# Cross-covariance attention with a mixture of adapters: gate weights and A in one tile, seven fillers fewer

## The chip, the cores and the metric

The kernel runs on one core of a Trainium2 chip. The metric is the device time of one execution in microseconds (us). Shown are the median of three runs and one execution taken by the hardware profiler. The engines are PE (TensorE, matrix products; PEld is its weight load), DVE (VectorE), ACT (ScalarE), POOL (GpSimd, which here mainly issues the loads) and SP (SyncE, which here issues the stores). Sixteen DMA engines move data.

## The reference

For each of 4 batches, q, k and v are 6400 x 256. The columns of q and k are normalised over the 6400 rows, a 256 x 256 attention comes out of them, and v is multiplied with it. Each of the 25600 result rows then goes through a mixture of 8 adapters of rank 16, of which the gate picks two.

```python
qn = q / (norm(q, axis=1) + 1e-6);  kn = k / (norm(k, axis=1) + 1e-6)
a  = softmax(kn.transpose(0, 2, 1) @ qn / tau)          # 4 x 256 x 256
x  = (v @ a).reshape(25600, 256)
logits = x @ w_gate                                     # 256 x 8
w  = softmax over the two largest logits of each row
out = x + sum over the two experts e: w_e * (x @ A[e]) @ B[e]
```

## The kernel before

Rows are handled in 50 chunks of 128 per batch; v comes in five tiles of ten chunks. The loads (q, k, v) turn fp32 into bf16 on the way and are issued by POOL in the fixed order of `WORDS`; SP issues the stores. A planner (`Plan`) simulates the engines with estimated costs and writes out a fixed order of steps for every engine, with the buffers that each step takes and gives back. Stores of the first batches are held back until given loads have landed (`HOLD`), so that loads go first.

Per batch there are three stages:

- G (lines 752 to 760): PE accumulates k'q and, for some groups of chunks, the squared norms. For the other groups (`OFF`) ACT squares and DVE adds up (`sq`, L775; `add`, L782; `red`, `n2p`).
- The attention: `n2`, `rsqrt`, `rq_ps`, `s`, `exp`, `aT_ps`, `aT`, then `waA_ps`. The last one multiplies the transposed attention with the gate weights (8 columns) and with A (128 columns: 8 experts of rank 16), so that each row of v needs one product for its logits and its adapter inputs. It is scaled into `waA_sb` by DVE (L910) and ACT (L908).
- The tiles of v: PE transposes (`T`, L942), `ZL` (L966) multiplies with `waA_sb` (136 columns), DVE works out the gate and its product with Z (`Ze`, L1044), PE transposes that (`gzT`, L1056), `Y` (L1069 and L1074) adds v times attention and the adapters' output, ACT and DVE copy the result to the y slots, and SP stores it.

The weights come from one step, `wts`, on DVE in the middle of the first batch: L677 copies A into a tile `a_raw` (per partition: expert, half of the 256 rows, rank), L680 the gate weights into a tile `wg_raw`, L682 scales B.

The fillers are steps `("warm", n)`, matmuls of 512 columns whose result nobody reads. The planner puts them into gaps of PE in the first batch; a number in `NO_WARM` is planned and then not emitted:

```python
def do_warm(s, n):
    if n in NO_WARM:
        return
```

Thirty are planned before PE's last real step; 12 are in `NO_WARM`, so 18 run. `keep_weights` drops a weight load if the same weights are already loaded and the load carries no semaphore, which is why the second matmul of a `waA_ps` pair has none in most cases.

Of the kernel before, what the change touches and what calls it, by code (L numbers as in the profile page):

```python
# [12 lines left out]
BF16 = mybir.dt.bfloat16  # L13
# [455 lines left out]
PARTS = {(0, 0): ((0, 5), (5, 12), (17, 8)), (0, 1): ((25, 17), (42, 8)), (3, 1): ((25, 17), (42, 8))}  # L469
REST, REST_AT, FULL, SIDE = (0, 1), 40, 112, 5  # L470
SLOTS = ((0, 4), (32, 34), (4, 6), (8, 12), (40, 42), (28, 32), (60, 62), (64, 68), (96, 98), (92, 96), (124, 126))
NO_WARM = {6, 7, 8, 9, 10, 11, 12, 25, 26, 27, 28, 29}
FINE = {3: ((0, 6), (6, 4)), 4: ((0, 4), (4, 4), (8, 2))}
SPLIT, SHARES = set(), ()
OFF = {(0, 0, 'k'), (0, 0, 'q'), (0, 1, 'k'), (0, 2, 'k'), (0, 2, 'q'), (0, 3, 'k'), (0, 4, 'k'), (0, 4,
# [102 lines left out]
def kernel(  # L578
# [11 lines left out]
    nc = tc.nc  # L590

    B, N, C = q.shape
    P = 128
    CC = C // P
    E = moe_w_gate.shape[1]
    R = moe_A.shape[2]
    ER = E * R
# [14 lines left out]
    const = ctx.enter_context(tc.tile_pool(name="const", bufs=1))  # L612
# [5 lines left out]
    W = {}  # L618
# [48 lines left out]
    def bank(s, name, shape, dtype):  # L667
        held["bank", name] = psum.tile(shape, dtype, tag=f"bank{at['bank', name]}", name=name[0] + "_ps")
        return held["bank", name]
# [2 lines left out]


    def do_wts(s):
        W["A"] = const.tile([P, E, CC, R], BF16, name="a_raw")
        for g in range(4):
            nc.vector.tensor_copy(W["A"][g * (P // 4):(g + 1) * (P // 4)], W["A0"][:, :, CC * g:CC * g + CC, :])  # L677
        W["wg"] = const.tile([P, CC, E], BF16, name="wg_raw")
        for g in range(4):
            nc.vector.tensor_copy(W["wg"][g * (P // 4):(g + 1) * (P // 4)], W["wg0"][:, g])  # L680
        W["B"] = const.tile([P, C], BF16, name="ball")
        nc.vector.tensor_scalar(out=W["B"], in0=W["B0"], scalar1=0.5, scalar2=None, op0=OP.mult)  # L682

# [206 lines left out]
    def do_waA_ps(s, b):  # L890
        ps = bank(s, ("waA", b), [P, CC, E + ER], FP32)
        for ic in range(CC):
            for cc in range(CC):
                lhsT = st[b]["aT"][:, cc, ic * P:(ic + 1) * P]
                nc.tensor.matmul(
                    ps[:, ic, 0:E], lhsT, W["wg"][:, cc, :],
                    start=(cc == 0 and ic == 0), stop=False, skip_group_check=True)
                nc.tensor.matmul(
                    ps[:, ic, E:E + ER], lhsT, W["A"][:, :, cc, :],
                    start=False, stop=(cc == CC - 1 and ic == CC - 1), skip_group_check=True)  # L900

    def do_waA(s, b, ic):
        if "waA" not in st[b]:
# [25 lines left out]
# [3 lines that stand above are left out]
        nc.tensor.matmul(bank(s, ("warm", n), [P, 512], FP32), W["ident"], W["ident"][:, None, :].to_broadcast([P, 4, P]),  # L932
                         start=True, stop=True)
# [146 lines left out]
    def do_store(s, b, i, c, n):  # L1080
# [3 lines left out]
        for rows in SHARES if (b, i) in SPLIT else (P,):  # L1084
            r = nc.sync.dma_start(out_v[b, p:p + rows, lo:lo + n, :], Y[p:p + rows, at_y:at_y + n, :])
            if (b, i) in HOLD and not p:
# [4 lines left out]


    do = dict(load=do_load, wts=do_wts, sq=do_sq, add=do_add, red=do_red, n2p=do_n2p, warm=do_warm, cast=do_cast, G=do_G, accs=do_accs, n2=do_n2, rsqrt=do_rsqrt, rq_ps=do_rq_ps, s=do_s,
              exp=do_exp, recip=do_recip, aT_ps=do_aT_ps, aT=do_aT, waA_ps=do_waA_ps, waA=do_waA,
              a=do_a, ZL=do_ZL, ZLe=do_ZLe, T=do_T, Te=do_Te, log=do_log, loge=do_loge, Z=do_Z, Ze=do_Ze, gzT=do_gzT,
              gzTe=do_gzTe, Y=do_Y, Ye=do_Ye, store=do_store)
# [55 lines left out]
```

## Time and profile before

| | |
|---|---|
| median of 3 runs | 251.62 us (251.37 to 251.63) |
| profiled execution, whole | 251.61 us |
| its span, first to last instruction | 247.2 us |
| mean granted clock of PE | 0.965 |
| busy, us | PE 215.3, DVE 185.4, ACT 169.6, POOL 27.4 |
| HBM read, written | 79.90 MB, 26.21 MB |
| waA_ps, 8 columns (L895) | 16 matmuls, 167 ns each in the middle |
| waA_ps, 128 columns (L898) | 16 matmuls, 216 ns each in the middle |
| fillers (L932) | 18 matmuls from 9.9 to 53.6 us, 13 weight loads |

The span holds the instructions only; the last transfers end after it. The duration of one matmul counts its way through the array, so matmuls in a row overlap, and what one costs is read from start to start. A window is a stretch of the span, with each engine's busy time and number of instructions in it, the clock that PE was granted (1.00 is full), and the DMA engines' mean busy share. Besides the printed views, the trace holds a record of every DMA packet with its queue, size, start and duration.

### The profile page before, as it was taken

How to read it: one execution, taken by the hardware profiler on the slowest of the kernel's cores; microseconds unless marked ns; L12 is line 12 of the kernel's file. 1: busy time of each engine (PE TensorE's matmuls, PEld its weight loads, DVE VectorE, ACT ScalarE, POOL GpSimd, SP SyncE). 2: the span in 40 equal slices, each digit the busy share in tenths (PEclk: the TensorE clock that was granted, in tenths of full speed). 3: DMA queues.
4: the chain of work that ended last, by engine and by line, in shares of the span. 5: the costliest groups of instructions: out<-in, count | busy, mean ns of one | idle time of the engine just before them, and what ended most of it. 6: DMA issues, size and time to landing. Idle time of an engine off the chain costs nothing.

```text
span 247.2 us, 5383 instructions
## 1 busy us (share of the span) xinstructions
PE 215.3 (87%) x2226; PEld 178.8 (72%) x2033; DVE 185.4 (75%) x514; ACT 169.6 (69%) x316; POOL 27.4 (11%) x61
## 2 busy tenths in 40 slices
PE   0657199398998999999969999999999999999995
PEld 0255077167777998978959787999775799999974
DVE  1145578467879789999974899998989588878780
ACT  3844442275666769888776787999443699888885
POOL 7800200200030011000201003110000000000000
PEclk9999869679999999999997999999999999999999
DMA  8999999999999999999999999999999999999999
GB/s 275 219 208 217 213 224 222 208 215 224 206 221 220 208 214 225 216 215 208 258 280 269 326 268 203 216 218 226 305 220 319 394 356 274 326 430 434 407 423 415
DMA packets 9157, 66.27 MB, mean 268 GB/s; under 512 B 1231, under 2 KB 1615, under 8 KB 5420
## 3 DMA queue, kind: packets, MB, share of 16 engines
q0 software_dynamic: 5872, 38.67, 75.2%
q1 hardware_dynamic: 2924, 26.47, 25.9%
q10 hardware_dynamic: 336, 0.79, 0.8%
q8 instruction: 17, 0.28, 0.4%
q14 instruction: 8, 0.07, 0.1%
HBM read 79.90 MB, written 26.21 MB: 429 GB/s over the span
## 4 chain that ended last, share of the span: by engine, by line
DMA 39%; PE 34%; DVE 11%; issue 9%; ACT 6%; POOL 1%; POOLq 0%; ACTq 0%
DMA v<-in_v_dram 27%; PE Y_ps L1069 10%; DMA qk<-in_q_dram 7%; PE Y_ps L1074 5%; PE ZL_ps L966 5%; DMA qk<-in_k_dram 5%; PE T_ps L942 5%; DVE ssq L782 4%; PE acc L752 3%; PE gzT_ps L1056 3%; DVE gz L1044 3%; ACT sq L775 3%; PE acc L756 2%; ACT y L922 1%; DVE y L924 1%
## 5 line engine op out<-in xcount | busy, mean ns | idle before, releaser
L752 PE MATMUL acc<-qk 128*128 128x256 bf16 (+1 forms) x400 | 75.7, 283 | 17.6 <-DMA qk<-in_k_dram 9.4
L782 DVE TENSOR_TENSOR ssq<-ssq,sq 128x1280 f32<-128x1280 f32 (+1 forms) x35 | 52.1, 1489 | 19.4 <-ACT sq L775 19.4
L752 PEld LDWEIGHTS <-qk 128*128 128x128 bf16 (+1 forms) x400 | 39.1, 103 | 31.8 <-DMA qk<-in_k_dram 11.5
L922 ACT COPY y<-Y_ps 128x512 f32<-128x512 f32 x87 | 50.7, 594 | 15.3 <-PE Y_ps L1074 13.0
L775 ACT ACTIVATE sq<-qk 128x1280 f32<-128x1280 bf16 (+1 forms) x35 | 44.8, 1280 | 23.3 <-DVE ssq L782 20.8
L1069 PE MATMUL Y_ps<-a_bf,vT 128*128 128x256 bf16 x400 | 60.0, 272 | 0.1
L1069 PEld LDWEIGHTS <-vT 128*128 128x128 bf16 x400 | 38.3, 98 | 5.1 <-issue 0.4
L1074 PE MATMUL Y_ps<-ball,gzT 128*128 128x256 bf16 x200 | 38.2, 273 | 0.0
L1044 DVE TENSOR_TENSOR gz<-zl,gatega 128x256 bf16<-128x256 f32 x95 | 35.5, 446 | 0.5
L756 PE MATMUL acc<-qk 128*128 128x128 bf16 (+1 forms) x170 | 32.6, 225 | 0.0
L942 PE MATMUL T_ps<-ident,v 128*128 128x128 f32 x200 | 26.9, 282 | 4.4 <-DMA v<-in_v_dram 4.1
L760 PE MATMUL acc<-qk 128*128 128x128 bf16 (+1 forms) x200 | 28.0, 222 | 0.0
L942 PEld LDWEIGHTS T_ps<-ident,v 128*128 128x128 f32 x200 | 22.6, 145 | 5.7 <-issue 4.3
L966 PE MATMUL ZL_ps<-waA_sb,vT 128*128 128x136 bf16 x380 | 26.3, 223 | 0.4 <-ACT y L922 0.3
L922 ACT COPY vT<-T_ps 128x512 f32<-128x512 f32 (+1 forms) x47 | 23.0, 546 | 5.2 <-PE T_ps L942 4.9
L966 PEld LDWEIGHTS <-vT 128*128 128x128 bf16 x380 | 23.8, 98 | 1.4 <-issue 0.4
L922 ACT COPY zl<-ZL_ps 128x408 f32<-128x408 f32 (+1 forms) x50 | 19.9, 457 | 3.5 <-PE ZL_ps L966 3.4
L1056 PE MATMUL gzT_ps<-ident,gz 128*128 128x128 f32 x100 | 20.0, 283 | 2.0 <-DVE gz L1044 1.9
L760 PEld LDWEIGHTS <-qk 128*128 128x128 bf16 (+1 forms) x200 | 18.5, 99 | 4.3
L1074 PEld LDWEIGHTS <-gzT 128*128 128x128 bf16 x200 | 19.5, 98 | 2.3
L924 DVE COPY zl<-ZL_ps 128x272 f32<-128x272 f32 (+1 forms) x26 | 12.7, 499 | 6.8 <-PE ZL_ps L966 6.6
L709 POOL DMA_DIRECT2D qk<-in_q_dram x11 | 6.2, 559 | 105.0 <-ACT y L922 41.3
(93 smaller groups left out, 226.1 us busy)
## 6 DMA issues: line engine op xcount, KB each, us to landing
out_dram<-y SPq DMA_DIRECT2D x10, 1280.0 KB, 11.0
out_dram<-y SPq DMA_DIRECT2D x4, 2560.0 KB, 17.6
v<-in_v_dram POOLq DMA_DIRECT2D x14, 640.0 KB, 27.4
qk<-in_q_dram POOLq DMA_DIRECT2D x5, 1600.0 KB, 16.4
qk<-in_k_dram POOLq DMA_DIRECT2D x5, 1600.0 KB, 23.4
v<-in_v_dram POOLq DMA_DIRECT2D x3, 1280.0 KB, 28.5
out_dram<-y SPq DMA_DIRECT2D x3, 512.0 KB, 5.0
qk<-in_q_dram POOLq DMA_DIRECT2D x1, 1088.0 KB, 18.2
```

The costliest lines, as they stand in the source:

```text
L752: nc.tensor.matmul(acc[ic][:, 0:256], kt[0:r, j, ic::CC], qt[0:r, j, :], start=c == 0, stop=False, skip_group_check=True)
L756: nc.tensor.matmul(acc[ic][:, 256:384], kt[0:r, j, ic::CC], kt[0:r, j, ic::CC], start=False, stop=False, skip_group_check=True)
L760: nc.tensor.matmul(acc[ic][:, 384:512], qt[0:r, j, ic * P:(ic + 1) * P], qt[0:r, j, ic * P:(ic + 1) * P], start=False, stop=c == NC - 1, s ...
L775: nc.scalar.activation(out[0:r, 0:n, :], t[0:r, j:j + n, :], ACT.Square)
L782: nc.vector.tensor_tensor(out=t, in0=t, in1=held["sq", (w, b, g), ""][0:r, 0:n, :], op=OP.add)
L922: nc.scalar.copy(out, in_)
L942: nc.tensor.matmul(ps[:, j, :], vt[:, c + j, :].bitcast(FP32), W["ident32"], is_transpose=True, start=(j == 0), stop=(j == n - 1))
L966: nc.tensor.matmul(ps[:, j, :], vT_of(b, i, c + j)[:, :, ic], st[b]["waA"][:, ic, :], start=(j == 0 and ic == 0), stop=(j == n - 1 and ic ...
L1044: nc.vector.tensor_tensor(out=pairs[:, h].rearrange("p c (e r) -> p c e r", e=E), in0=z[:, 2 * h:2 * h + 2, :].rearrange("p c (e r) -> p c ...
L1056: nc.tensor.matmul(ps[:, j, :], pairs[:, j * P:(j + 1) * P], W["ident32"], is_transpose=True, start=(j == 0), stop=(j == n // 2 - 1))
L1069: nc.tensor.matmul(ps[:, j, :], vT_of(b, i, c + j)[:, :, ic], st[b]["a"][:, ic, :], start=(j == 0 and ic == 0), stop=False, skip_group_che ...
L1074: nc.tensor.matmul(ps[:, j, :], pair[:, :, j], W["B"], start=False, stop=(j == 1), skip_group_check=True)
```

## The change

The tiles for A and the gate weights become one tile `wgA` with, for each half of the rows, 8 columns of the gate and then 128 of A. The copies of `wts` write into parts of it. In `waA_ps` the two matmuls of each step become one of 136 columns. `NO_WARM` gets the numbers 0 to 5 and 24, so that 11 fillers run. The planner's costs and its order stay.

```diff
-NO_WARM = {6, 7, 8, 9, 10, 11, 12, 25, 26, 27, 28, 29}
+NO_WARM = {0, 1, 2, 3, 4, 5, 6, 7, 8, 9, 10, 11, 12, 24, 25, 26, 27, 28, 29}
...
     def do_wts(s):
-        W["A"] = const.tile([P, E, CC, R], BF16, name="a_raw")
+        W["wgA"] = const.tile([P, CC, E + ER], BF16, name="wga_raw")
         for g in range(4):
-            nc.vector.tensor_copy(W["A"][g * (P // 4):(g + 1) * (P // 4)], W["A0"][:, :, CC * g:CC * g + CC, :])
-        W["wg"] = const.tile([P, CC, E], BF16, name="wg_raw")
+            rows = slice(g * (P // 4), (g + 1) * (P // 4))
+            nc.vector.tensor_copy(W["wgA"][rows, :, E:].rearrange("p cc (e r) -> p e cc r", e=E),
+                                  W["A0"][:, :, CC * g:CC * g + CC, :])
         for g in range(4):
-            nc.vector.tensor_copy(W["wg"][g * (P // 4):(g + 1) * (P // 4)], W["wg0"][:, g])
+            nc.vector.tensor_copy(W["wgA"][g * (P // 4):(g + 1) * (P // 4), :, 0:E], W["wg0"][:, g])
...
                 lhsT = st[b]["aT"][:, cc, ic * P:(ic + 1) * P]
                 nc.tensor.matmul(
-                    ps[:, ic, 0:E], lhsT, W["wg"][:, cc, :],
-                    start=(cc == 0 and ic == 0), stop=False, skip_group_check=True)
-                nc.tensor.matmul(
-                    ps[:, ic, E:E + ER], lhsT, W["A"][:, :, cc, :],
-                    start=False, stop=(cc == CC - 1 and ic == CC - 1), skip_group_check=True)
+                    ps[:, ic, :], lhsT, W["wgA"][:, cc, :],
+                    start=(cc == 0 and ic == 0), stop=(cc == CC - 1 and ic == CC - 1), skip_group_check=True)
```

## The prediction

> **What bounds the kernel.** I read the page first: the busy shares, the slices, the queues.
>
> ```profile
> span 247.2 us, 5383 instructions
> ...
> PE 215.3 (87%) x2226; PEld 178.8 (72%) x2033; DVE 185.4 (75%) x514; ACT 169.6 (69%) x316; POOL 27.4 (11%) x61
> ...
> DMA  8999999999999999999999999999999999999999
> ...
> q8 instruction: 17, 0.28, 0.4%
> ```
>
> No compute engine is full, but the DMA row is 9 in all slices but the first. So the 16 DMA engines are the bound. The chain of waits agrees up to 130 us (DMA v 27.1%, most of it there) and names PE after that, up to "244.64 0.59 ACT y L922". Which of the two sets the end shows in the windows of the last microseconds (PE, PEld, DVE, ACT, POOL busy, then clock, DMA share, GB/s):
>
> ```profile
> 245.00:245.50 0.50, 0.00 (x0) 0.00 (x0) 0.00 (x0) 0.23 (x1) 0.00 (x0) 1.00 0.97 393
> ...
> 247.50:248.00 0.50, 0.00 (x0) 0.00 (x0) 0.00 (x0) 0.00 (x0) 0.00 (x0) 0.50 0.96 381
> 248.00:248.50 0.50, 0.00 (x0) 0.00 (x0) 0.00 (x0) 0.00 (x0) 0.00 (x0) 0.50 0.81 315
> 248.50:249.00 0.50, 0.00 (x0) 0.00 (x0) 0.00 (x0) 0.00 (x0) 0.00 (x0) 0.50 0.26 98
> 249.00:249.50 0.50, 0.00 (x0) 0.00 (x0) 0.00 (x0) 0.00 (x0) 0.00 (x0) 0.50 0.05 20
> 249.50:250.00 0.50, 0.00 (x0) 0.00 (x0) 0.00 (x0) 0.00 (x0) 0.00 (x0) 0.50 0.03 12
> ```
>
> The last store is issued at 245.25, and the DMA engines stay full until 248: PE could end some 0.1 us earlier or later and nothing would move. From 249.0 the share is 0.05, one engine of sixteen (0.06). The time hangs on that engine.
>
> Its story is in the trace's packet records (a packet starts where the one before it on the same engine ended). Fifteen engines finish their part of the last store between 247.87 and 248.93; one finishes at 249.77. That one had a store boundary at 244.06 and the next, eight packets on, at 246.62: 2.56 us, where the others need 1.25. In between lies a 16 KB packet of queue q8, from 244.84 to 245.81: the last of the 17 instruction fetches of the page. So this fetch cost its engine 2.56 - 1.25 = 1.31 us, and without it that engine would have ended at 249.77 - 1.31 = 248.46, inside the pack.
>
> The profiled execution took 251.61 us, 1.84 more than the last packet's end on the span's clock; the median of the runs shown is 251.62, so sums made against the one hold for the other. About 0.2% (0.5 us) is what a measurement can tell from no change.
>
> **Part 1: one matmul of 136 columns.** Now a pair of matmuls with one weight load:
>
> ```profile
> 202.71 0.17 PE L895 MATMUL waA_ps<-wg_raw,aT_sb 128*128 128x8 bf16 x1
> 202.74 0.22 PE L898 MATMUL waA_ps<-a_raw,aT_sb 128*128 128x128 bf16 x1
> 202.80 0.17 PE L895 MATMUL waA_ps<-wg_raw,aT_sb 128*128 128x8 bf16 x1
> ...
> 203.04 0.57 PE L966 MATMUL ZL_ps<-waA_sb,vT 128*128 128x136 bf16 x7
> ```
>
> From start to start four pairs take 0.33 us (202.71 to 203.04). The nearest row for the merged one is ZL, also 136 columns with a weight load each: 20 in 1.18 us, 0.059 each, so four take 0.24. Bounds: 0.057 (128 columns, L760) to 0.083 (the pair, no gain). Saved: 0.09 us per batch, 0.38 in all. At 203 it lies on PE's chain, which runs without a gap to 244.6, so the last store is issued 0.09 us earlier, into DMA queues that are full until 248. Worth nothing: the cover is those full queues; if the stores kept up with PE, it would be worth 0.09.
>
> **Part 2: the copies.** The same eight DVE casts (L677 four at 0.282 us, L680 four at 0.165) now write rows of 136. Element counts stay; the A copies still write runs of 16, so I take no change. A faster copy has no reason, and the upper bound is a_bf (L916), 256 scattered elements in 0.69 us: +0.4 each, +1.6 us at 33.58. Behind them on DVE are the sums of squares up to 41.88, and behind those n2p on PE and the load that POOL issues at 42.68. That load's first packet comes at 53.5, and the first q load needed 3.9 us from issue to packet (1.44 to 5.32), so 53.5 - 42.68 - 3.9 = 6.9 us of cover. DVE itself then waits 2.23 us for ACT (acc_sb), which waited for a landing at 43.2. So nothing of it reaches the end. No wait, DMA or queue order is added.
>
> **Part 3: the fillers.** Of 18 fillers in the trace (L932) go the six at 9.85 to 12.39 and the last at 53.62. The last frees 0.22 us of PE; PE then idles at 61.0 for 1.2 us anyway. What the six do is in windows cut at the clock's steps (its changes lie at 11.59, 28.66, 35.49, 45.72, 52.55: multiples of 3.41 apart; the 1.00 before 11.59 only means that no record came earlier, since 256 columns took 0.21 us there, half speed):
>
> ```profile
> 8.18:11.59 3.41, 3.40 (x14) 1.58 (x11) 0.00 (x0) 3.41 (x3) 3.10 (x5) 1.00 1.01 207
> 11.59:15.01 3.42, 1.96 (x18) 1.08 (x15) 1.49 (x1) 1.15 (x2) 0.99 (x2) 1.00 1.05 213
> ...
> 28.66:32.07 3.41, 1.84 (x12) 0.94 (x8) 1.49 (x1) 1.85 (x2) 0.00 (x0) 0.50 1.05 215
> 32.07:35.49 3.42, 3.42 (x23) 2.35 (x18) 3.20 (x10) 1.33 (x2) 0.00 (x0) 0.50 1.07 223
> ```
>
> A window with 3.4 us of PE raised the clock at its end, one with 1.84 didn't. Without the six, 8.18:11.59 holds 2.1 us (the ten G matmuls), so the clock stays at half until 18.42, after a full window. By then PE has done 2.3 of the 3.6 us of G work that begins at 13.85; the rest ends at 19.7 instead of 17.4, the work fed at 18.72 at 22.0 instead of 21.0, the side rows at 24.4 instead of 23.6. PE next waits for a load until 30.23, and the only load that waits for these buffers (POOL, 26.78) is released by ACT at 26.5. Cost: nothing, with 2 us of cover or more. "TensorE: Matmul & The Clock Gate" (the section on why it matters for kernels) speaks against the removal: it asks for no PE gap over about 3 us between bursts; by it the slow stretch costs, and the rows above say that the cost ends in front of a DMA wait.
>
> **Part 4: what is left, the length of PE's stream.** 16 matmuls go, with three second weight loads (L898 PEld x3), seven fillers and three weight loads of theirs (the six have two, the last one its own): 29 of PE's 4314 records (2226 matmuls, 2033 weight loads, 54 semaphore instructions, a drain). The 17 fetches come 257 records apart on average: 202 records had started at the first, 4314 at the last, (4314 - 202) / 16. So fetches follow the stream, and the 17th came when PE had 38 records less than 17 * 256 = 4352. "Runtime: NRT & Kernel Launch" (Instruction fetch mechanics) gives 256 instructions per block, which agrees, and calls a crossing "mostly hidden"; by that rule part 4 is worth 0, while the tail above shows 0.84 us not hidden.
>
> Say fetch n is asked for when record 256n - o is reached. PE stood at record 202 from 23.4 to 30.2 while the first packet came at 24.95, so o is 54 or more, or less if PE's front reads ahead of a matmul that waits. With o = 54 the delays from asking to packet have a median of 1.5 us, with 67 of 2.1, with 90 of 3.3; the nearest measured delay, a store's issue to its first packet, is 3.4 to 3.6 us (116.93 to 120.48), so I stop at 90. The new stream ends at 4314 - 29 = 4285, the 17th request is at 4352 - o: beyond the end if o is below 67. Then PE ends, drains, and waits with the rest for the stores, and the fetch is gone or comes too late to matter. DMA then ends at the next engine's 248.93: **249.77 - 248.93 = 0.84 us off**, 250.8.
>
> **The rivals.**
> - A, the fetch falls out: 251.61 - 0.84 = 250.8; with the scatter of the runs (0.26) 250.5 to 251.1. For it: record 4352 already lies 38 past the end of the old stream, and will lie 67 past the end of the new one.
> - B, it still comes, 29 records later, at some 20 records per us 1.4 us later, at 246.3. Its engine still has work until 248.46, so it pays 1.31 again: 251.6, no change. This holds for o of 67 to 90, and for a front that reads on past PE's end.
> - C, it comes on another engine, of those that end at 248.2 to 248.93: end 249.5 to 250.24, 251.3 to 252.1.
> - D, the slower side: the fillers did hold the clock. If PE stays at half from 13.85 on, G ends at 48.7 instead of 42.05; the 42.68 load has its 6.9 us, but the attention and the first tile start 3.5 us late, and with one more half window (1.7 us) 5.2. They release the load that POOL issues at 70.02, whose first packet is due at 77.7: cover 77.7 - 70.02 - 3.9 = 3.8 us. It decides from a slip of 3.8 us on, price up to 1.4, middle 0.8: 252.4. Against it: from 30.23 G alone, without fillers, brought the clock back at 35.49.
>
> **How the numbers follow.** o between 54 and 67 is about a third of 54 to 90; reading ahead (o lower) adds to A unless the front also passes PE's last wait. I give A 0.48, B 0.32, C 0.10, D 0.10. The forecast is A's 250.8. Range 250.5 to 252.1: it holds A, B and C and leaves D out. Faster by over 0.2% is A without its upper edge: 0.46; slower is D with a rest of B and C: 0.13; within 0.2%: 0.41. A's own range is 250.5 to 251.1.
>
> **What would show it.** Right: q8 with 16 packets (0.26 MB) in the page, DMA share 0.00 after 249.0, PE 2203 matmuls, one waA row of 136 columns at 0.06 us start to start, half clock at 13.85 with G done before 30.23. B shows as 17 packets and again one engine (0.05) up to 249.7; C as 17 with another end. Wrong altogether: a DMA share below 0.9 for several us around 53 or 77, which would be D, or a tail set by PE.

## The result, and the profile after

The kernel after takes 250.66 us (median of six runs, 250.52 to 251.01), the kernel before 251.64 us in six runs beside it (251.37 to 251.92). The ratio is 0.9961, with a 95% interval of 0.9949 to 0.9974: 0.98 us, or 0.4%, faster. The profiled execution took 250.69 us, 0.92 less than that of before. The forecast was 250.8.

The page of the kernel after, the lines that answer to those of before:

```profile
span 245.0 us, 5349 instructions
...
PE 213.6 (87%) x2203; PEld 178.1 (73%) x2024; DVE 185.4 (76%) x514; ACT 169.0 (69%) x316; POOL 27.6 (11%) x61
...
DMA  8999999999999999999999999999999999999999
...
q8 instruction: 16, 0.26, 0.4%
```

The DMA row is as full as before, DVE, ACT and POOL are as busy as before, and the queue of instruction fetches has 16 packets where it had 17. PE has 23 matmuls and 9 weight loads less. The last windows (PE, PEld, DVE, ACT, POOL busy, then clock, DMA share, GB/s):

```profile
245.00:245.50 0.50, 0.00 (x0) 0.00 (x0) 0.00 (x0) 0.00 (x0) 0.00 (x0) 1.00 0.98 401
247.50:248.00 0.50, 0.00 (x0) 0.00 (x0) 0.00 (x0) 0.00 (x0) 0.00 (x0) 0.68 0.96 385
248.00:248.50 0.50, 0.00 (x0) 0.00 (x0) 0.00 (x0) 0.00 (x0) 0.00 (x0) 0.50 0.85 328
248.50:249.00 0.50, 0.00 (x0) 0.00 (x0) 0.00 (x0) 0.00 (x0) 0.00 (x0) 0.50 0.18 66
249.00:249.50 0.50, 0.00 (x0) 0.00 (x0) 0.00 (x0) 0.00 (x0) 0.00 (x0) 0.50 0.00 0
```

Up to 248.5 this is, within 0.04 of the DMA share, the table of before. The 0.05 and 0.03 that one engine gave from 249.0 on are gone: the last packet ends at 249.015 instead of 249.771, 0.76 us earlier. The rest of the 0.92 us is what lies behind the last packet: 250.69 - 249.02 = 1.67 us here, 1.84 before.

The two edits themselves, in the rows of the timeline (start, us from first start to last end, engine, line, operation) and of the windows cut at the clock's steps:

```profile
201.21 0.40 PE L896 MATMUL waA_ps<-wga_raw,aT_sb 128*128 128x136 bf16 x4
201.45 1.35 PE L964 MATMUL ZL_ps<-waA_sb,vT 128*128 128x136 bf16 x20
```

```profile
15.26 0.63 PE L753 MATMUL acc<-qk 128*128 128x256 bf16 x2
15.68 0.42 PE L761 MATMUL acc<-qk 128*128 128x128 bf16 x2
15.90 0.63 PE L753 MATMUL acc<-qk 128*128 128x256 bf16 x2
...
19.49 0.38 PE L753 MATMUL acc<-qk 128*128 128x256 bf16 x2
19.70 0.28 PE L761 MATMUL acc<-qk 128*128 128x128 bf16 x2
19.82 0.38 PE L753 MATMUL acc<-qk 128*128 128x256 bf16 x2
```

```profile
12.16:15.57 3.41, 1.57 (x10) 1.26 (x11) 1.53 (x2) 1.27 (x1) 0.55 (x1) 1.00 1.03 208
15.57:18.98 3.42, 3.42 (x21) 2.62 (x20) 2.08 (x2) 1.27 (x1) 0.00 (x0) 1.00 1.12 218
18.98:22.40 3.42, 3.42 (x40) 3.06 (x37) 2.08 (x2) 1.27 (x1) 0.00 (x0) 1.00 1.05 217
```

The four merged matmuls take 0.24 us from start to start (201.21 to 201.45). Without the early fillers the same four matmuls of G take 0.64 us from start to start at 15.26 and 0.33 at 19.49, and PE gets through 21 matmuls in the full window before 18.98 and 40 in the one behind it: it ran at half speed until then. (The clock column says 1.00 for the early windows in both kernels; it has no record there.)

### The profile page after: what moved, and what is told of

Its sections match the earlier page's. It is cut to its first block, busy times and chain, and to the rows that moved or that the text cites. A ratio compares the mean times of both kernels' runs of the same rounds, so it can differ in the third digit from the quotient of the medians.

```text
span 245.0 us, 5349 instructions
## 1 busy us (share of the span) xinstructions
PE 213.6 (87%) x2203; PEld 178.1 (73%) x2024; DVE 185.4 (76%) x514; ACT 169.0 (69%) x316; POOL 27.6 (11%) x61
## 4 chain that ended last, share of the span: by engine, by line
DMA 39%; PE 37%; DVE 9%; issue 8%; ACT 6%; POOL 1%; POOLq 0%; ACTq 0%
DMA v<-in_v_dram 27%; PE Y_ps L1067 11%; DMA qk<-in_q_dram 7%; PE Y_ps L1072 5%; PE ZL_ps L964 5%; PE T_ps L940 5%; DMA qk<-in_k_dram 5%; DVE ssq L783 4%; PE acc L753 4%; PE gzT_ps L1054 3%; ACT sq L776 3%; DVE gz L1042 2%; PE acc L757 2%; ACT y L920 1%; POOL qk L710 1%
## 5 line engine op out<-in xcount | busy, mean ns | idle before, releaser
L753 PE MATMUL acc<-qk 128*128 128x256 bf16 (+1 forms) x400 | 77.5, 290 | 18.1 <-DMA qk<-in_k_dram 9.6
L753 PEld LDWEIGHTS <-qk 128*128 128x128 bf16 (+1 forms) x400 | 39.9, 105 | 31.0 <-DMA qk<-in_k_dram 10.3
L757 PE MATMUL acc<-qk 128*128 128x128 bf16 (+1 forms) x170 | 32.6, 225 | 0.0
L940 PE MATMUL T_ps<-ident,v 128*128 128x128 f32 x200 | 25.8, 274 | 4.5 <-DMA v<-in_v_dram 4.2
L761 PE MATMUL acc<-qk 128*128 128x128 bf16 (+1 forms) x200 | 28.7, 227 | 0.0
L940 PEld LDWEIGHTS T_ps<-ident,v 128*128 128x128 f32 x200 | 21.7, 141 | 5.8 <-issue 4.4
L761 PEld LDWEIGHTS <-qk 128*128 128x128 bf16 (+1 forms) x200 | 19.1, 102 | 4.9
```

Of the source, the lines that this page charges most:

```text
L753: nc.tensor.matmul(acc[ic][:, 0:256], kt[0:r, j, ic::CC], qt[0:r, j, :], start=c == 0, stop=False, skip_group_check=True)
L757: nc.tensor.matmul(acc[ic][:, 256:384], kt[0:r, j, ic::CC], kt[0:r, j, ic::CC], start=False, stop=False, skip_group_check=True)
L761: nc.tensor.matmul(acc[ic][:, 384:512], qt[0:r, j, ic * P:(ic + 1) * P], qt[0:r, j, ic * P:(ic + 1) * P], start=False, stop=c == NC - 1, s ...
L940: nc.tensor.matmul(ps[:, j, :], vt[:, c + j, :].bitcast(FP32), W["ident32"], is_transpose=True, start=(j == 0), stop=(j == n - 1))
```

## The experiments

**What is in question.** The theory from the tail of the trace: the 17th instruction fetch made one DMA engine late, and the kernel after is faster only because its PE stream is too short to ask for that fetch. The rivals: PE has less to do, or ends earlier; the fillers, and with them the clock, matter; the merged matmul matters on the path.

The runs use the edits in `NO_WARM` and a pad, matmuls of one column into a PSUM bank that nobody reads, put in the place of a filler that isn't emitted:

```diff
     def do_warm(s, n):
+        if n == 0:
+            ps = bank(s, ("warm", n), [P, 512], FP32)
+            for x in range(33):
+                nc.tensor.matmul(ps[:, x % 512:x % 512 + 1], W["ident"], W["ident"][:, 0:1],
+                                 start=True, stop=True)
+            return
         if n in NO_WARM:
             return
```

**The stream's length alone.** e1: the kernel after, with that pad, in time in which PE waits for a load (10.45 to 11.46 us), so that its stream is as long as that of before, to one record.

> The changed kernel with 33 one-column matmuls and two weight loads on PE at 10 us, where PE is idle: PE's stream has 4315 records again (4314 before, 4280 changed). Fetch theory: 17 packets in q8, the last near 244, one DMA engine alone after 249.0, time back to 251.6 (ratio 0.999 to 1.002). Rival, the saved PE work counts: 33 columns in idle time cost nothing, 250.7 (ratio 0.996), whatever q8 says.

Measured: 251.79 us (251.57 to 252.09, 11 runs) against 251.88 of before (29 runs beside it); ratio 0.9996 (0.9987 to 1.0004). One microsecond of idle PE time, filled at 10 us, takes back the whole gain. The windows at the end:

```profile
249.00:249.50 0.50, 0.00 (x0) 0.00 (x0) 0.00 (x0) 0.00 (x0) 0.00 (x0) 0.50 0.09 37
249.50:250.00 0.50, 0.00 (x0) 0.00 (x0) 0.00 (x0) 0.00 (x0) 0.00 (x0) 0.50 0.05 20
250.00:250.50 0.50, 0.00 (x0) 0.00 (x0) 0.00 (x0) 0.00 (x0) 0.00 (x0) 0.50 0.03 12
```

The 17th fetch is back (its packet at 243.17), and so is one engine at a share of 0.05, up to 250.28. PE's last matmul began at 242.56 in this run, 1.8 us before that of the kernel before: PE's end doesn't set the time.

**The shorter stream by another way.** e2: the kernel before, with its pairs and two tiles, but no filler at all.

```diff
-NO_WARM = {6, 7, 8, 9, 10, 11, 12, 25, 26, 27, 28, 29}
+NO_WARM = set(range(30))
```

> The kernel before (pairs of matmuls stay) with none of the 18 fillers: 4279 records, one fewer than the changed kernel. Fetch theory: 16 packets in q8, last DMA packet near 249.0, 250.7 (ratio 0.995 to 0.998). Rival, the saved PE work counts: nothing of the merge is in it, so 251.5 or, where the fillers held the clock, slower: 251.6 to 253.0.

Measured: 250.81 us (250.78 to 251.19); ratio 0.9965 (0.9953 to 0.9978). Without the merged matmul it is as fast as the kernel after: 16 packets on q8, last DMA packet at 249.39.

```profile
q8 instruction: 16, 0.26, 0.4%
```

```profile
249.00:249.50 0.50, 0.00 (x0) 0.00 (x0) 0.00 (x0) 0.00 (x0) 0.00 (x0) 0.50 0.04 16
249.50:250.00 0.50, 0.00 (x0) 0.00 (x0) 0.00 (x0) 0.00 (x0) 0.00 (x0) 0.50 0.00 0
```

**Each half alone.** e3: the kernel after with the old `NO_WARM`. e4: the kernel before with the new one.

> The merged matmul with all 18 fillers: 4295 records. Fetch theory: time follows q8, 250.7 with 16 packets, 251.6 with 17; by my o of 54 to 90 the limit is somewhere between 4281 and 4298 records, so either can come. Rival, saved PE work: 0.09 us per batch at most, 251.3 to 251.6, whatever q8 says.

> Only the seven fillers gone, pairs of matmuls stay: 4299 records. Fetch theory: time follows q8, 251.6 with 17 packets (likelier), 250.7 with 16. Rival, the fillers matter by PE work or clock: 251.4 without them, or up to 252.4 if they held the clock, whatever q8 says.

Measured: both fall into two groups. e3: two runs at 250.73 and 250.75, nine from 251.46 to 252.44 (median 251.65, ratio 0.9992, 0.998 to 1.0005). e4: four runs from 250.75 to 251.09, eight from 251.37 to 252.04 (median 251.56, ratio 0.9985, 0.9975 to 0.9996). The groups lie where the times with and without the 17th fetch lie. So neither half brings the gain surely, and the same program can fall on either side. That its faster runs did without the 17th fetch is read from their times alone: one run of each kernel has a trace, and those of e3 and e4 are slower ones. The profiled run of e3 was of the slower group (251.78), and its page shows 16 packets; the packet records have the 17th, at 250.81, behind the stores:

```profile
248.50:249.00 0.50, 0.00 (x0) 0.00 (x0) 0.00 (x0) 0.00 (x0) 0.00 (x0) 0.50 0.27 102
249.00:249.50 0.50, 0.00 (x0) 0.00 (x0) 0.00 (x0) 0.00 (x0) 0.00 (x0) 0.50 0.02 8
249.50:250.00 0.50, 0.00 (x0) 0.00 (x0) 0.00 (x0) 0.00 (x0) 0.00 (x0) 0.50 0.00 0
250.00:250.50 0.50, 0.00 (x0) 0.00 (x0) 0.00 (x0) 0.00 (x0) 0.00 (x0) 0.50 0.00 0
250.50:251.00 0.50, 0.00 (x0) 0.00 (x0) 0.00 (x0) 0.00 (x0) 0.00 (x0) 0.50 0.15 33
```

The stores were through at 249.17, as in the kernel after. Then 1.6 us of nothing, and a fetch. The run ended 251.78 - 249.17 = 2.61 us behind the last store, where the kernel after needs 1.67: a fetch that comes too late for the stores is paid behind them, 0.94 us.

**Where the edge lies.** e5 and e6: the kernel after with pads of 4 and of 9 (each brings two weight loads with it), 4286 and 4291 records where the kernel after has 4280.

> The changed kernel with four one-column matmuls and two weight loads more: 4286 records. The padded kernel of 4315 and the ones of 4295 and 4299 fell back to 251.6 in most runs; in the one of 4295 the 17th fetch came at 250.81, after the stores, and the end waited for it. Theory: a request that falls behind PE's last wait is paid in full at the end, one that falls behind the whole program isn't. 4286 lies between: 250.7 with 16 packets if its request still falls behind the program, 251.6 with a 17th after 250. Rival, only a fetch that delays the stores counts, and the slow runs of 4295 were such: 250.7.

> The same with nine one-column matmuls: 4291 records. Late-fetch theory: the limit lies between 4280 and 4295, so 4291 is likelier past it than 4286: 251.4 to 251.8 with a fetch after 250; 250.7 with 16 packets otherwise. Rival, only a fetch among the stores counts: 250.7.

Measured: e5 again in two groups, six runs from 250.59 to 250.92 and four from 251.59 to 252.16 (median 250.90, ratio 0.9976, 0.9958 to 0.9993); its profiled run (251.59) is of the slower group and has the late fetch, at 250.77. e6: 251.81 us, all ten runs above 251.5 (ratio 0.9999, 0.9989 to 1.0009), with the fetch at 244.91. So with such pads the edge lies some 6 records above the kernel after. Request 17 comes at record 4352 - o; with the edge at about 4286, o is about 66, an estimate. The number of records alone doesn't place the edge: 4291 had no fast run in ten, while 4295 (e3) had two in eleven and 4299 (e4) four in twelve.

**No fillers at all.** e7: the kernel after with `NO_WARM = set(range(30))`, 4260 records.

> The changed kernel without the 11 fillers that it kept: 4260 records, a weaker clock between 42 and 53. Fetch theory: still 16 fetches, 250.7, nothing more to win. Rival, every PE record less is worth something: 20 records less than 4280, at 0.9 us for the 34 of the change, would give 250.2. Clock theory: the kept fillers shorten the first attention, slower without, 251 to 252.

Measured: 250.72 us (median of seven runs, 250.58 to 251.20; an eighth, at 263.72, is not counted); ratio 0.9955 (0.9944 to 0.9967). No gain and no loss against the kernel after's 0.9961: the eleven fillers that are left do nothing for the time. PE's last matmul began at 244.29 here, 1.5 us later than in the kernel after, and the stores were through at 249.23: once more PE's end is not the bound.

**One fetch more.** e8: the kernel after with pads of 153 (n = 0) and 136 (n = 6), 4573 records and 18 fetches.

> The changed kernel with 289 one-column matmuls in PE's idle time of the first batch (153 at 10 us, 136 at 24 us): 4573 records, so 18 fetches, the last again near the end. Fetch theory: the end is that of the latest engine, so 18 fetches cost what 17 do if the 18th comes to another engine: 251.6 to 251.9; 253.0 if to the same. Rival, each fetch delays the whole (1.31 us on one of sixteen engines, or about 0.9 each): 252.5. The matmuls themselves are hidden: G is late by 0.5 us at 14 and early enough for the load at 30.

Measured: 251.66 us (251.43 to 252.02); ratio 0.9993 (0.9983 to 1.0003). The 18th fetch comes at 244.71, where the 17th of before did, and 18 cost no more than 17.

```profile
248.50:249.00 0.50, 0.00 (x0) 0.00 (x0) 0.00 (x0) 0.00 (x0) 0.00 (x0) 0.50 0.47 184
249.00:249.50 0.50, 0.00 (x0) 0.00 (x0) 0.00 (x0) 0.00 (x0) 0.00 (x0) 0.50 0.10 41
249.50:250.00 0.50, 0.00 (x0) 0.00 (x0) 0.00 (x0) 0.00 (x0) 0.00 (x0) 0.50 0.11 41
```

But the share is 0.10 where one engine gave 0.05: by the packet records two engines end at 249.94 and 249.96, and the next one at 248.99.

**Is it the place of the fetch, or its number?** Up to here it could be that a fetch costs only if it falls among the last stores. e9 and e10 put the 17th far ahead of them: pads of 150 (n = 0), and of 150 and 45 (n = 0 and 6).

> The kernel after with 150 one-column matmuls and two weight loads more in idle PE time of the first batch: 4432 records on PE, so 17 fetches again (record 4352 is passed), but the 17th is asked for 118 records earlier than in the kernel before, and its packet is expected near 238 us, while all sixteen engines still have several us of loads and stores ahead. Theory (a fetch costs only where its engine can no longer give the work to the others' pace, in the last stores): about 250.8 us, +-0.3, with DMA share 0.00 after 249.3. Rival 1 (every fetch costs its engine 1.3 us to the end of the kernel, wherever it lies near the end): 251.6 to 251.8, like the kernel before. Rival 2 (the number of fetches counts, 17 against 16): also 251.6 to 251.8.

> The same with 195 one-column matmuls: 4479 records on PE, 17 fetches, the 17th asked for 165 records before the end of the stream that the kernel before has, packet expected near 236 us. Theory (only a fetch in the last stores, or behind them, costs): 250.8 +-0.3. Rival (the count, or any late fetch): 251.6 to 251.8. Between the two: if e9 is slow and this one fast, the fetch's engine needs more than about 10 us to catch up, and the boundary lies between 236 and 238 us.

Measured: 251.78 us both (251.31 to 252.21 and 251.44 to 252.22); ratios 0.9999 (0.999 to 1.0008) and 1.0000 (0.9991 to 1.0009). The theory missed: the fetch lay at 236.87 and at 236.49, and cost as much as at 244.84. In e9 its packet took 0.96 us and the 10 KB packet behind it 0.74 instead of 0.39, 1.31 us together, and thirteen us later one engine is still late:

```profile
248.50:249.00 0.50, 0.00 (x0) 0.00 (x0) 0.00 (x0) 0.00 (x0) 0.00 (x0) 0.50 0.30 115
249.00:249.50 0.50, 0.00 (x0) 0.00 (x0) 0.00 (x0) 0.00 (x0) 0.00 (x0) 0.50 0.06 25
249.50:250.00 0.50, 0.00 (x0) 0.00 (x0) 0.00 (x0) 0.00 (x0) 0.00 (x0) 0.50 0.06 25
250.00:250.50 0.50, 0.00 (x0) 0.00 (x0) 0.00 (x0) 0.00 (x0) 0.00 (x0) 0.50 0.06 25
```

A steady 0.06 is one engine of sixteen, up to 250.54. The packet records suggest why it doesn't catch up: between 10 and 240 us all sixteen engines have a packet under way all the time, in before, after, e9 and e10 alike, and the packets of q0 (the loads) take 185.8 us per engine in each of them. The data packets of every size come in multiples of sixteen, which fits a fixed share for each engine. So no engine has a pause to make up a loss in, and in e9 and e10 what it lost at 236 it still lacks at the end.

That leads to a new theory: sixteen fetches hit sixteen engines once each, in turn, and delay them alike; the 17th and 18th hit an engine a second time.

**Fifteen and nineteen.** e12 leaves out ten of the fifty chunks of G in every batch (its transfers are all there):

```diff
         acc = st[b]["acc"]
+        if c < NC - 1 and c % 5 == 3:
+            return
         (qt, j), (kt, _) = qk_of("q", b, c), qk_of("k", b, c)
```

e11 is the kernel after with pads of 180, 190, 110 and 60 (n = 0, 6, 18, 21); the last two stand in place of fillers that ran.

> The kernel after without the part of G that the chunks 3, 8, 13 and so on of each batch give (ten of fifty; their loads stay, the output differs): 4006 records on PE, 274 less, so 15 fetches. All transfers are those of the kernel after, and PE has less to do. Theory (fetches in turn over sixteen engines): one engine is early by one fetch and the others set the end as before: 250.7 us, like after, within 0.3. Rival 2 (each fetch costs time, and the last most): 249.4 to 249.9. Rival 3 (PE's end sets the time after all): some 2.5 us of PE work gone in every batch, 249 or less.

> The kernel after with 540 one-column matmuls (and four weight loads) more, spread over four stretches in which its PE waits or runs fillers: 4822 records on PE, so 19 fetches (4352 + 512 - about 64 is passed, 4352 + 768 isn't). New theory after e9 and e10, whose 17th fetch lay 8 us ahead of PE's end and cost the same: every engine is busy from the first load to the last store and cannot make a loss good, each fetch takes one engine about 1.3 us, and the fetches go round the sixteen engines in turn, so that sixteen delay all alike, and the 17th, 18th and 19th each make one engine late by one more fetch. So: 251.7 us, no more than with 17 or 18, and a DMA share of about 3/16 = 0.19 in the stretch where one engine gave 0.06 and two gave 0.10 to 0.11. Rival 1 (the fetches fall on engines at random): three late engines at most, but with sixteen fetches some engine would have had two as well, and here one may have three: up to 253. Rival 2 (each further fetch costs time): 252.5 to 253.

e12 measured: 250.94 us (250.81 to 251.16), ratio 0.9967 (0.9955 to 0.9979): as with sixteen, though PE has 274 records and 11 us of work less.

```profile
PE 202.5 (82%) x2049; PEld 168.1 (68%) x1904; DVE 185.5 (76%) x514; ACT 168.3 (69%) x316; POOL 27.6 (11%) x61
...
q8 instruction: 15, 0.25, 0.4%
```

The packet records have one engine that is early: it ends at 247.20, the next at 247.97, the middle at 248.70. So with one fetch less than sixteen one engine is early and the time doesn't move, as the new theory says; and PE's work is not the bound. (The early engine alone is weak evidence: e9, with 17 fetches, has one that ends at 247.75, the next at 248.31.)

e11 measured: 252.77 us (252.67 to 254.65), ratio 1.0064 (1.0037 to 1.009), slower than both. That is not the 251.7 of the new theory but the 252.5 to 253 of rival 2, and the picture isn't three late engines either: seven end between 249.96 and 251.11, and the middle of the sixteen, 248.52 to 248.71 in the other kernels, is 249.22. Something else went with it: in the packet records e11 alone of the fourteen kernels has engines without a packet in mid-kernel (1.2 engine-microseconds between 70 and 80, 0.8 between 90 and 100), so some load was issued late, and its q0 packets took 186.6 us per engine instead of 185.8. The pads at 48 and 52 us lie ahead of the first attention on PE, which fits a late load, but that was not traced through. For the number of fetches e11 decides nothing: neither the new theory nor rival 2 is shown by it.

**All runs by the packet records.** "Middle" is the median over the sixteen engines of the end of their last store. "Run" is the time of the profiled execution, to which the row belongs.

| kernel | fetches | last fetch at | PE's last matmul | middle | last engines | run |
|---|---|---|---|---|---|---|
| e12 | 15 | 232.84 | 243.35 | 248.70 | 249.32 | 250.99 |
| after | 16 | 232.09 | 242.75 | 248.54 | 249.02 | 250.69 |
| e2 | 16 | 231.89 | 242.72 | 248.62 | 249.39 | 251.09 |
| e7 | 16 | 234.41 | 244.29 | 248.58 | 249.23 | 250.90 |
| e3 | 17 | 250.81 | 242.46 | 248.61 | 249.17 | 251.78 |
| e5 | 17 | 250.77 | 242.71 | 248.59 | 249.13 | 251.59 |
| before | 17 | 244.84 | 244.33 | 248.52 | 249.77 | 251.61 |
| e1 | 17 | 243.17 | 242.56 | 248.58 | 250.28 | 252.09 |
| e4 | 17 | 243.46 | 242.63 | 248.57 | 249.74, 250.33 | 252.04 |
| e6 | 17 | 244.91 | 244.04 | 248.59 | 250.46 | 252.20 |
| e9 | 17 | 236.87 | 242.56 | 248.62 | 250.54 | 252.21 |
| e10 | 17 | 236.49 | 242.70 | 248.64 | 250.55 | 252.22 |
| e8 | 18 | 244.71 | 244.37 | 248.71 | 249.94, 249.96 | 251.70 |

The execution ends 1.67 to 1.84 us behind the last engine in every row but those of e3 and e5 (2.61 and 2.46), where the fetch stands behind the stores: the time follows the last engine, run by run. PE's end wanders over 1.9 us without any effect; the middle stays within 0.2 us; the last engine is 0.5 to 0.8 us behind the middle where up to sixteen fetches come before the stores are through (e3 and e5 among them), and 1.25 to 1.9 us with more. The profiled runs of e1, e6, e9 and e10 are the slowest of theirs; by the medians the 17th fetch costs about 1 us. e4 does not fit the plain count: it has a second engine 1.2 us behind with 17 fetches.

**What stays open.** That the fetches go round the engines in turn is inferred from these ends: the records don't name an engine, and no engine can be followed through the whole run. The durations of the fetch packets speak for a fixed order: in the kernel before the first eight took 975, 974, 961, 893, 893, 948, 945 and 921 ns, the next eight 974, 974, 961, 893, 879, 934, 931 and 925, and the 17th 968. They can't tell a round of eight from one of sixteen. Why e4 shows a second late engine, and why kernels of 4286, 4295 and 4299 records are sometimes fast and sometimes slow while the one of 4291 was slow ten times, was not settled. And whether sixteen fetches together cost their 1.3 us as well (all engines late alike) was not tried: it would need a PE stream without fetches.

## Why the prediction was right

- **The bound and the last engine.** Right: the table shows that the time follows the last DMA engine, and e1 and e7 that PE's end doesn't matter.
- **Part 1.** The 0.059 us per merged matmul, from the ZL row, was 0.060, and worth nothing at the end, as e2 shows, which lacks it.
- **Part 2.** The copies take 0.282 and 0.166 us, as before. Right, and the bound of +1.6 us was not used.
- **Part 3.** Half speed lasted to 18.98 (18.42 foreseen), that G stretch ended at 24.3 (24.4), and PE next waited for a load until 30.68. e7 shows that the other fillers don't count either. Rival D is out.
- **Part 4.** The saving was sized as the gap to the next engine, 0.84 us; the last packet moved 0.76, because the next engine ended at 249.02 and not at 248.93, and the execution moved 0.92. The stream was sized 29 records shorter and became 34 shorter. The merge took the 19 that were foreseen (e3, 4295 against 4314); the seven fillers took 15 instead of 10 (e4, 4299), with three weight loads more and two semaphore instructions. This was luck: 4285 records would have stood at the very edge, beside e5's 4286, where four runs of ten pay.
- **The step that failed** is the half sentence "the fetch is gone or comes too late to matter". A fetch can come late and matter: in e3 and e5 it stands behind the last store, and the run ends 2.6 and 2.5 us behind the store instead of 1.7. The case "a front that reads on past PE's end" was put under B with the right time, but with the price inside the stores, where these fetches don't fall.
- **What was right by a reason too narrow.** The text read the 1.31 us as the price of a fetch in the tail. e9 and e10 show the same price at 236.5, where the engines have no pause in which to catch up. The rule of the Trainium skill, "Runtime: NRT & Kernel Launch" (Instruction fetch mechanics), that crossing a block is "mostly hidden", holds here for the sixteenth, as e12 shows no gain from one crossing less than after, and not for the 17th, which is paid in full.
- **Not foreseen:** PE's last matmul began 1.6 us earlier, not 0.1. In the kernel before, the clock was 0.50 from 131.06 to 134.47 with PE busy throughout; half of that window is 1.7 us. The trace of after has no such window there:

```profile
131.06:134.47 3.41, 3.41 (x18) 3.17 (x17) 1.05 (x3) 2.22 (x6) 1.05 (x2) 0.50 0.97 251
```

```profile
131.60:135.00 3.40, 3.40 (x44) 3.05 (x39) 2.10 (x5) 3.40 (x8) 1.06 (x2) 1.00 1.02 267
```

Before, e6, e7 and e8 have such a window, and their last matmul begins at 244.04 to 244.37; after, e1 to e5, e9 and e10 have none, and theirs begins at 242.46 to 242.75. Both kinds occur with sixteen fetches and with seventeen, so it is not put down to the change. Had PE set the end, a comparison of single traces would have credited the change with it.
- **The chances.** A had 0.48 because o was open between 54 and 90; e5 and e6 put it near 66, just on A's side of the 67 that the text gave as the edge.

## What to carry to other kernels

When the DMA engines are full from the first load to the last store, look at each engine's end and not at their mean share: one late engine of sixteen is the time, and what an engine loses to an instruction fetch it may not make up (here not in thirteen us). There the length of an instruction stream can have steps: here nine one-column matmuls in idle time, with two weight loads (e6), cost the 0.4% that the change had won. Before crediting an edit with such a gain, give the dropped instructions back as idle padding; here that took the whole gain away, while the edit that looked like the point of the change was worth nothing.

## What the runs showed of the hardware

- One instruction fetch of 16 KB takes its DMA engine 0.88 to 1.07 us while data is under way (all fourteen traces), and made it 1.31 us late in all (before, between two store boundaries; e9, with the slowed packet behind it). By the medians kernels with a seventeenth fetch ahead of or among the last stores take about 1 us more than those with fifteen or sixteen (251.6 to 251.8 against 250.7 to 250.9); an eighteenth adds nothing (e8, 251.66).
- A last fetch can come 1.6 us behind the stores, and the execution then ends 0.8 to 0.9 us later (e3 and e5, fetch at 250.81 and 250.77).
- The same program can be fast in one run and slow in the next, at 4286, 4295 and 4299 records of PE (e5, e3, e4); that it is the last fetch that is made or not is inferred from the times.
- Changes of PE's granted clock lie multiples of 3.41 us apart, at another phase in each trace (28.66 in before, 29.23 in after). A window at half clock at 131 us goes with a last matmul 1.3 to 1.9 us later, and with no change of the time.
